# Accumulating products of a seven-product block in shared PSUM banks, with neighbouring blocks interleaved

## The chip, the cores and the metric

The kernel runs on one core of a Trainium2 chip. The metric is the time of one execution on the device in microseconds (us); lower is better. TensorE multiplies matrices into PSUM banks, VectorE and ScalarE do elementwise work and read PSUM, GpSimd does elementwise work in SBUF, and SyncE (SP) issues most of the transfers.

## The reference

Sliding-window attention (4 batches, 8 heads, 576 positions, window 64), and behind it two feed-forward parts on its 2,304 tokens. The change concerns only the second one's first product, which makes h.

```python
a = x @ w1;  b = x @ w2              # x: 2304 x 512 from attention
y = ((a * b) @ w3) @ w_out           # 2304 x 512
h = y @ w_in                         # 2304 x 2048
g = np.maximum(0.01 * h, h)
return g @ w_out2                    # 2304 x 512
```

## The kernel before, in words

Each float32 operand is split into a high part (fp32r) and a remainder, and `mm3` makes a product of three matmuls: high by high, high by low, low by high. Attention, the first feed-forward part and the loading of weights take the first half of the execution. y is kept transposed in DRAM (`yd`), and so is h (`hd`).

The stage of this study makes h. It is cut into 24 blocks (`Quad(p, c)`): p counts 8 pairs of 128 rows of features of h, c counts 3 pairs of 384 tokens. A block is a 2 x 2 product of submatrices, and it is made with seven products instead of eight, from sums and differences of the submatrices. `w_ops(p)` makes the seven weight operands (L553), `y_ops(c, j)` the seven operands of y (L527): loads, differences on VectorE, a cast to the high part on ScalarE (L574, L542), a subtraction for the low part on VectorE or, for the last c, on GpSimd (L575, L543). Blocks run in the order (0,0), (1,0), (2,0), (0,1), ... for the first three p, and then by p.

A product (`Quad.product`) is six matmuls of 128x128 by 128x384 into a PSUM bank of its own; eight banks take turns (six in `ps2`, two in `ps_h`). Then `Quad.add` carries the product to where it belongs: product 1 is copied by ScalarE (L608) into an SBUF tile `c`, and each other one is added by VectorE to a tile `c` (L610), seven additions in a block. Four tiles of a block are results, c11, c12, c21 and c22, and go to `hd` by SP (L615). The products come in the order 1, 6, 2, 7, 4, 5, 3. They are kept in their order on TensorE by `tc.issue_after(pss["pr"])`. On the other engines the order of the instructions is laid down when the kernel is built, by a scheduler with priorities (`first()` puts an instruction ahead) and its own estimate of times; each engine then runs its list strictly in order, and what is ready waits behind what is not.

Between products other work is put on the engines: `advance` takes the last weight matrix through its steps, two calls in a block while it lasts, of which ScalarE's part is a rescaling (L293, `f` from `raw`) that is put behind the last copy. `feed` loads the next piece on SP behind the last store of h. `w_ops` of a later p stands behind the fourth product of a block. After block 21 the pool `yb0` is released, and loads and splits for the last stage begin (`ahead`, L259, L693).

## Time and profile before

| what | us |
|---|---|
| median of three runs | 864.32 |
| runs | 864.15, 864.32, 867.67 |
| span of the profiled execution | 866.3 |
| TensorE busy, whole span | 821.0 |
| VectorE busy | 574.1 |
| ScalarE busy | 391.1 |
| granted clock of TensorE, mean | 0.988 |

The profile gives the span from the first to the last instruction of one execution. That execution's own time is not told apart from the three runs; 867.67, the only one above the span, has 1.4 us around it. TensorE's matmuls overlap: each is shown with 0.33 us in h's stage while the next starts after 0.17, so a wait shows as a larger distance between starts.

### The profile page before, as it was taken

The numbers are of one execution on the slowest core, as the hardware profiler recorded it, in microseconds if no ns is written. First come the engines' busy times: TensorE is split into PE (matmuls) and PEld (weight loads), VectorE is DVE, ScalarE is ACT, GpSimd is POOL, SyncE is SP. The second block draws the span as 40 slices with busy tenths as digits, with TensorE's granted clock in tenths as the row PEclk, the third lists the DMA queues.
The fourth block names the chain that finished last, engine by engine and source line by source line (L and its number), as shares of the span: only waits on it lengthen the run. The fifth ranks groups of instructions, "written<-read, shape, count | busy, mean of one in ns | idle before, by whom it ended". The sixth has DMA issues, their size and how long they took to land. (4 is left out here: it accounts for less than half of the span.)

```text
span 866.3 us, 15325 instructions
## 1 busy us (share of the span) xinstructions
PE 821.0 (95%) x5332; PEld 751.5 (87%) x5332; DVE 574.1 (66%) x1419; ACT 391.1 (45%) x988; POOL 82.8 (10%) x91
## 2 busy tenths in 40 slices
PE   5789799999999999999999799998999999999997
PEld 4577699999999999999999699997998888888885
DVE  6799996553655377657614987988768655555552
ACT  6687973333333254435324412322215545555552
POOL 1012551110111011100000330000000000000000
PEclk9999999999999999999999999999999999999999
DMA  8798787673546367874202447896638335344341
GB/s 248 198 218 237 198 204 197 152 156 76 130 107 147 68 158 194 242 223 134 77 29 64 147 156 254 284 287 227 209 130 284 112 98 158 105 130 131 98 129 45
DMA packets 203693, 139.44 MB, mean 161 GB/s; under 512 B 137312, under 2 KB 181856, under 8 KB 203616
## 3 DMA queue, kind: packets, MB, share of 16 engines
q1 hardware_dynamic: 199008, 133.74, 54.5%
q10 hardware_dynamic: 4608, 4.72, 1.7%
q8 instruction: 42, 0.69, 0.3%
q14 instruction: 35, 0.29, 0.1%
HBM read 94.63 MB, written 43.78 MB: 160 GB/s over the span
## 5 line engine op out<-in xcount | busy, mean ns | idle before, releaser
L75 PE MATMUL ab<-x,w 128*128 128x288 f32 x512 | 154.1, 301 | 4.8 <-ACT x L235 3.3
L76 PE MATMUL ab<-x,w 128*128 128x288 f32 x512 | 152.1, 297 | 0.0
L77 PE MATMUL ab<-x,w 128*128 128x288 f32 x512 | 152.1, 297 | 0.0
L75 PE MATMUL pr<-yop,w 128*128 128x384 f32 x324 | 111.0, 343 | 10.3 <-DVE c L610 7.3
L75 PE MATMUL o<-w,g 128*128 128x512 f32 x288 | 113.4, 394 | 0.5 <-ACT w L259 0.3
L76 PE MATMUL o<-w,g 128*128 128x512 f32 x288 | 113.1, 393 | 0.0
L77 PE MATMUL pr<-yop,w 128*128 128x384 f32 x324 | 109.5, 338 | 0.0
L76 PE MATMUL pr<-yop,w 128*128 128x384 f32 x324 | 109.4, 338 | 0.0
L75 PEld LDWEIGHTS ab<-x,w 128*128 128x128 f32 x512 | 97.1, 190 | 6.6 <-ACT x L235 3.5
L610 DVE TENSOR_TENSOR c<-pr,c 128x384 f32<-128x384 f32 x168 | 87.5, 551 | 18.7 <-PE pr L77 17.7
L76 PEld LDWEIGHTS ab<-x,w 128*128 128x128 f32 x512 | 97.2, 190 | 0.2
L77 PEld LDWEIGHTS ab<-x,w 128*128 128x128 f32 x512 | 97.1, 190 | 0.1
L694 DVE TENSOR_TENSOR t<-h,t 128x384 f32<-128x384 f32 x96 | 53.5, 558 | 49.2 <-ACT t L693 49.1
L77 PE MATMUL o<-w,g 128*128 128x512 f32 x288 | 82.8, 393 | 0.0
L75 PE MATMUL mm<-ab,wf 128*128 128x288 f32 x256 | 76.5, 310 | 0.0
L693 ACT ACTIVATE t<-h 128x384 f32<-128x384 f32 x96 | 50.5, 526 | 57.6 <-DVE g L696 55.0
L293 ACT ACTIVATE f<-raw 128x512 f32<-128x512 f32 x72 | 48.6, 674 | 60.7 <-DMA raw<-in_moe_w_out_dram 25.5
L77 PE MATMUL mm<-ab,wf 128*128 128x288 f32 x256 | 74.8, 294 | 0.0
L76 PE MATMUL mm<-ab,wf 128*128 128x288 f32 x256 | 74.6, 293 | 0.0
L75 PEld LDWEIGHTS pr<-yop,w 128*128 128x128 f32 x324 | 61.3, 189 | 14.8 <-DVE c L610 10.0
L696 DVE TENSOR_TENSOR g<-t,g 128x384 fp32r<-128x384 f32 x96 | 53.4, 557 | 28.0 <-ACT g L695 27.7
L192 POOL TENSOR_TENSOR s<-s,rs 128x384 f32<-128x384 f32 x48 | 41.5, 865 | 292.2 <-DVE rs L191 202.7
(100 smaller groups left out, 1541.1 us busy)
## 6 DMA issues: line engine op xcount, KB each, us to landing
hd<-c SPq DMA_DIRECT2D x96, 192.0 KB, 2.6
h<-hd SPq DMA_DIRECT2D x96, 192.0 KB, 2.4
raw<-in_moe_w_dram SPq DMA_DIRECT2D x32, 512.0 KB, 4.6
raw<-in_moe_w_out_dram SPq DMA_DIRECT2D x24, 512.0 KB, 4.8
raw<-in_moe_w_in_dram SPq DMA_DIRECT2D x16, 512.0 KB, 4.9
wd<-f SPq DMA_DIRECT2D x32, 256.0 KB, 3.3
f<-wd SPq DMA_DIRECT2D x32, 256.0 KB, 3.9
vt<-in_v_dram SPq DMA_DIRECT2D x56, 128.0 KB, 2.8
```

What stands on the lines that cost most here:

```text
L75: pe.matmul(ps, lhsT=lh, rhs=rh, start=first, stop=False)
L76: pe.matmul(ps, lhsT=lh, rhs=rl, start=False, stop=False)
L77: return pe.matmul(ps, lhsT=ll, rhs=rh, start=False, stop=last).ins
L192: pool.tensor_tensor(out=s, in0=s, in1=rs.unsqueeze(2).to_broadcast([P, GT, P]), op=ALU.mult)
L293: act.mul(u["f"], u["hi"].bitcast(F32), 2.0 ** -112)
L610: dve.tensor_tensor(out=self.sb[to], in0=ps, in1=self.sb[of], op=ALU.add)
L693: act.mul(t, h, 0.01)
L694: dve.tensor_tensor(out=t, in0=h, in1=t, op=ALU.max)
L696: dve.tensor_tensor(out=g[:, 1], in0=t, in1=f32(g[:, 0]), op=ALU.subtract)
```

## The change

Products 1, 6, 5 and 3 of a block now go one after the other into one bank (a) without clearing it, and ScalarE copies the partial sum out after each: 1 for c11, 1+6 for c21, 1+6+5 for c22, 1+6+5+3 for c12. Products 7 and 4 share a second bank (b), and product 2 has its own (c). VectorE adds three times in a block: 2 to c11, 7 to c22, 7+4 to c21. A product that writes on in a bank has to wait until the copy before it has been read out. The steps of neighbouring blocks are interleaved: seven product slots in a block, `ORDER` gives the slot of each step counted from the block's first, so that the sequence is 1, 2, 3 of the block before, 6, 7, 4 of the block before, 5. `w_ops` is called behind the fifth step and its last part behind the sixth; the weight tiles of p = 3 and 6 take the place of those of p = 0. `yb0` is released behind the last step of block 21.

```diff
@@ -71,10 +71,10 @@
 
         return tc.high_priority(offset=3000)
 
-    def mm3(ps, lh, ll, rh, rl, first, last):
-        pe.matmul(ps, lhsT=lh, rhs=rh, start=first, stop=False)
-        pe.matmul(ps, lhsT=lh, rhs=rl, start=False, stop=False)
-        return pe.matmul(ps, lhsT=ll, rhs=rh, start=False, stop=last).ins
+    def mm3(ps, lh, ll, rh, rl, first, last, more=False):
+        pe.matmul(ps, lhsT=lh, rhs=rh, start=first, stop=False, skip_group_check=more)
+        pe.matmul(ps, lhsT=lh, rhs=rl, start=False, stop=False, skip_group_check=more)
+        return pe.matmul(ps, lhsT=ll, rhs=rh, start=False, stop=last, skip_group_check=more).ins
 
     const = ctx.enter_context(tc.tile_pool(name="const", bufs=1))
     wpool = tc.alloc_tile_pool(name="wpool", bufs=1)
@@ -543,12 +543,12 @@
             (pool if c == NP - 1 else dve).tensor_tensor(out=t[:, i, j, 1], in0=x, in1=f32(t[:, i, j, 0]), op=ALU.subtract)
 
     def w_tile(p, j):
-        m = 1 if j == 3 else 2
-        if p:
-            return ph.tile([P, m, 2, 2 * P], F32R, name=f"w{j}", tag=f"w{j}", bufs=2)
+        shape = [P, 1 if j == 3 else 2, 2, 2 * P]
+        if p % 3 or p and j == 2:
+            return ph.tile(shape, F32R, name=f"w{j}", tag=f"w{j}", bufs=2)
         if j == 2:
-            return stage.tile([P, m, 2, 2 * P], F32R, name="raw", tag="raw", bufs=RAW)
-        return yb0.tile([P, m, 2, 2 * P], F32R, name=f"w{j}", bufs=1)
+            return stage.tile(shape, F32R, name="raw", tag="raw", bufs=RAW)
+        return yb0.tile(shape, F32R, name=f"w{j}", tag=f"w{j}", bufs=1)
 
     def w_ops(p):
 
@@ -564,9 +564,9 @@
         s1, s2, s3, s4 = (sums[i // 2][:, i % 2] for i in range(4))
         src = (u[1].rearrange("p k c m -> p c k m"), sums[0], sums[1], a11.unsqueeze(1))
         add, sub = ALU.add, ALU.subtract
-        ops = {}
-        for j, todo in ((3, ()), (1, ((s1, a21, a22, add), (s2, s1, a11, sub))), (0, ()),
-                        (2, ((s3, a11, a21, sub), (s4, a12, s2, sub)))):
+        ops = wop[p] = {}
+
+        def part(j, todo):
             for o, x0, x1, op in todo:
                 dve.tensor_tensor(out=o, in0=x0, in1=x1, op=op)
             t = w_tile(p, j)
@@ -575,7 +575,11 @@
             dve.tensor_tensor(out=l, in0=src[j], in1=f32(h), op=sub)
             for i in range(t.shape[1]):
                 ops[2 * j + i] = t[:, i]
-        wop[p] = ops
+
+        part(3, ())
+        part(1, ((s1, a21, a22, add), (s2, s1, a11, sub)))
+        part(0, ())
+        return lambda: part(2, ((s3, a11, a21, sub), (s4, a12, s2, sub)))
 
 
 
@@ -583,31 +587,39 @@
 
     n_of["bank"] = 0
 
+    def bank():
+
+        n_of["bank"] += 1
+        pool = ps_h if n_of["bank"] % 8 in (1, 2) else ps2
+        return pool.tile([P, DM], F32, name="pr")[:, 0:NB2]
+
     class Quad:
+
+        ORDER = (("a", 1, 0), ("c", 2, 1), ("a", 6, 3), ("b", 7, 4), ("a", 5, 6), ("a", 3, 9), ("b", 4, 12))
+
         def __init__(self, p, c):
             self.p, self.c = p, c
-            self.sb = {}
-
-        def product(self, m):
-            n_of["bank"] += 1
-            pool = ps_h if n_of["bank"] % 8 in (1, 2) else ps2
-            ps = pool.tile([P, DM], F32, name="pr")[:, 0:NB2]
+            self.sb, self.ps = {}, {}
+
+        def product(self, at, m):
+
+            new = at not in self.ps
+            if new:
+                self.ps[at] = bank()
             a, b = PRODUCTS[m]
             w, y = wop[self.p][a], yop[self.c]
             with tc.issue_after(pss["pr"]):
                 for j in range(2):
                     ws = slice(P * j, P * j + P)
-                    pss["pr"] = mm3(ps, w[:, 0, ws], w[:, 1, ws], y[:, b, j, 0], y[:, b, j, 1], j == 0, j == 1)
-            return ps
-
-        def add(self, to, ps, of):
-
-            if to not in self.sb:
-                self.sb[to] = ph.tile([P, NB2], F32, name="c", tag="c", bufs=8)
-            if of is None:
-                pss["copy"] = act.copy(self.sb[to], ps).ins
-            else:
-                dve.tensor_tensor(out=self.sb[to], in0=ps, in1=self.sb[of], op=ALU.add)
+                    pss["pr"] = mm3(self.ps[at], w[:, 0, ws], w[:, 1, ws], y[:, b, j, 0], y[:, b, j, 1], new and j == 0, j == 1, not new)
+            return self.ps[at]
+
+        def keep(self, to, ps):
+            self.sb[to] = ph.tile([P, NB2], F32, name="c", tag="c", bufs=8)
+            pss["copy"] = act.copy(self.sb[to], ps).ins
+
+        def add(self, to, ps):
+            dve.tensor_tensor(out=self.sb[to], in0=ps, in1=self.sb[to], op=ALU.add)
 
         def out(self, n):
             fh, th = int(n[1]) - 1, int(n[2]) - 1
@@ -615,14 +627,22 @@
             pss["store"] = sp.dma_start(hd[:, 2 * self.p + fh, t0:t0 + NB2], self.sb.pop(n)).ins
 
         def step(self, k):
-            m, adds, done = ((1, [("c11", None)], []), (6, [("c12", "c11")], []), (2, [("c11", "c11")], ["c11"]),
-                             (7, [("c22", "c12")], []), (4, [("c21", "c22")], ["c21"]),
-                             (5, [("c12", "c12"), ("c22", "c22")], ["c22"]), (3, [("c12", "c12")], ["c12"]))[k]
-            ps = self.product(m)
-            for to, of in adds:
-                self.add(to, ps, of)
-            for n in done:
-                self.out(n)
+
+            at, m, _ = self.ORDER[k]
+            ps = self.product(at, m)
+            if k in (0, 2, 4, 5):
+                self.keep({0: "c11", 2: "c21", 4: "c22", 5: "c12"}[k], ps)
+            if k == 1:
+                self.add("c11", ps)
+                self.out("c11")
+            if k == 4:
+                self.add("c22", self.ps["b"])
+                self.out("c22")
+            if k == 5:
+                self.out("c12")
+            if k == 6:
+                self.add("c21", ps)
+                self.out("c21")
 
     ysteps = []
     for b in range(B):
@@ -654,7 +674,7 @@
             ps_h = tc.alloc_tile_pool(name="ps_h", bufs=2, space=PSUM, side="right", reuse_waits="tile")
             yb0 = tc.alloc_tile_pool(name="yb0", bufs=1, side="right", reuse_waits="tile")
             yop[0] = yb0.tile([P, 7, 2, 2, NB2], F32R, name="yop")
-            early = [lambda: w_ops(0), lambda: y_ops(0, 0), lambda: y_ops(0, 1)]
+            early = [lambda: w_ops(0)(), lambda: y_ops(0, 0), lambda: y_ops(0, 1)]
     for e in ysteps:
         y_step(*e)
 
@@ -738,33 +758,35 @@
     FIRST = 3
     order = [(p, c) for c in range(NP) for p in range(FIRST)] + [(p, c) for p in range(FIRST, NF) for c in range(NP)]
     quads = [Quad(p, c) for p, c in order]
-    w_ops(1)
-    for i, q in enumerate(quads):
-        for k in range(7):
+    w_ops(1)()
+    slots_h = sorted((7 * i + Quad.ORDER[k][2], i, k) for i in range(len(quads)) for k in range(7))
+    for _, i, k in slots_h:
+        with first():
+            quads[i].step(k)
+        if k == 3 and order[i] == (NF - 2, NP - 1):
             with first():
-                q.step(k)
-            if k == 3 and order[i] == (NF - 2, NP - 1):
-                with first():
-                    for f in range(WLEAD):
-                        load_w(f)
-            if k in (1, 4) and i >= FIRST * (NP - 1) and n_of["fin"] < len(units):
-                if n_of["cap"] == KEPT:
-                    n_of["cap"], n_of["room"] = len(units), 3
-                    feed()
-                else:
-                    advance(len(units))
-            if k == 0 and i < FIRST * (NP - 1) and i % FIRST == 0:
-                c = i // FIRST + 1
-                yop[c] = ph.tile([P, 7, 2, 2, NB2], F32R, name=f"yop{c}", bufs=1)
-            if k == 3:
-                if i == 0:
-                    w_ops(2)
-                elif i < FIRST * (NP - 1) and i % FIRST in (1, 2):
-                    y_ops(i // FIRST + 1, i % FIRST - 1)
-                p = order[i][0] + 2 if order[i][1] == NP - 1 else 0
-                if FIRST <= p < NF:
-                    w_ops(p)
-        if order[i] == (NF - 1, 0):
+                for f in range(WLEAD):
+                    load_w(f)
+        if k in (1, 4) and i >= FIRST * (NP - 1) and n_of["fin"] < len(units):
+            if n_of["cap"] == KEPT:
+                n_of["cap"], n_of["room"] = len(units), 3
+                feed()
+            else:
+                advance(len(units))
+        if k == 0 and i < FIRST * (NP - 1) and i % FIRST == 0:
+            c = i // FIRST + 1
+            yop[c] = ph.tile([P, 7, 2, 2, NB2], F32R, name=f"yop{c}", bufs=1)
+        if k == 3:
+            if i == 0:
+                w_ops(2)()
+            elif i < FIRST * (NP - 1) and i % FIRST in (1, 2):
+                y_ops(i // FIRST + 1, i % FIRST - 1)
+        p = order[i][0] + 2 if order[i][1] == NP - 1 else 0
+        if k == 4 and FIRST <= p < NF:
+            rest = w_ops(p)
+        if k == 5 and FIRST <= p < NF:
+            rest()
+        if k == 6 and order[i] == (NF - 1, 0):
             yb0.release()
             po1 = tc.alloc_tile_pool(name="po1", bufs=4, side="right", reuse_waits="tile")
             for n in range(LOADS):
```

## Rows read from the trace of the kernel before

**Rows 1.** Timeline of TensorE, single rows: start, us taken, instruction, [idle before, releaser].

```profile
468.08 0.34 PE L75 MATMUL pr<-yop,w 128*128 128x384 f32 x1
...
476.55 0.34 PE L75 MATMUL pr<-yop,w 128*128 128x384 f32 x1
...
497.99 0.45 PE L75 MATMUL pr<-yop,w 128*128 128x384 f32 x1 [0.93 <-DVE c L610]
...
505.45 0.45 PE L75 MATMUL pr<-yop,w 128*128 128x384 f32 x1
...
579.43 0.33 PE L75 MATMUL pr<-yop,w 128*128 128x384 f32 x1
...
615.45 0.34 PE L75 MATMUL pr<-yop,w 128*128 128x384 f32 x1
...
659.24 0.34 PE L77 MATMUL pr<-yop,w 128*128 128x384 f32 x1
```

**Rows 2.** Stretches A to D: length, busy PE, PEld, DVE, ACT, POOL; PE clock, DMA share, GB/s.

```profile
468.10:505.50 37.40, 31.63 (x171) 28.70 (x169) 34.30 (x59) 19.66 (x43) 14.80 (x13) 1.00 0.48 153
505.50:549.40 43.90, 43.90 (x253) 43.90 (x253) 33.31 (x68) 9.02 (x17) 1.28 (x2) 1.00 0.68 229
549.40:615.40 66.00, 61.48 (x338) 59.92 (x337) 58.03 (x121) 17.29 (x32) 0.00 (x0) 0.97 0.82 262
615.40:659.40 44.00, 44.00 (x254) 43.86 (x252) 31.10 (x60) 11.63 (x24) 0.00 (x0) 1.00 0.55 181
```

**Rows 3.** Groups by line in h's stage: instructions, busy us, mean ns, idle before.

```profile
L75 PE MATMUL pr<-yop,w 128*128 128x384 f32 x324 | 111.0, 343 | 10.3 <-DVE c L610 7.3 <-ACT c L608 2.1 <-ACT io L520 0.9
...
L610 DVE TENSOR_TENSOR c<-pr,c 128x384 f32<-128x384 f32 x164 | 85.5, 551 | 18.7 <-PE pr L77 17.7 <-ACT f L293 0.4
...
L608 ACT COPY c<-pr 128x384 f32<-128x384 f32 x24 | 11.4, 474 | 39.4 <-PE pr L77 36.6 <-DMA hd<-c 2.8
```

**Rows 4.** Timeline of TensorE: a product's end, two waits, a longer matmul.

```profile
506.43 0.33 PE L77 MATMUL pr<-yop,w 128*128 128x384 f32 x1
...
555.24 0.44 PE L75 MATMUL pr<-yop,w 128*128 128x384 f32 x1 [0.45 <-ACT c L608]
...
605.42 0.44 PE L75 MATMUL pr<-yop,w 128*128 128x384 f32 x1 [2.09 <-DVE c L610]
...
607.29 0.53 PE L77 MATMUL pr<-yop,w 128*128 128x384 f32 x1
```

**Rows 5.** Timeline of ScalarE in the same stage, single rows.

```profile
485.78 0.47 ACT L608 COPY c<-pr 128x384 f32<-128x384 f32 x1
...
503.12 0.47 ACT L608 COPY c<-pr 128x384 f32<-128x384 f32 x1
...
506.81 0.48 ACT L608 COPY c<-pr 128x384 f32<-128x384 f32 x1 [1.33 <-PE pr L77]
...
554.72 0.47 ACT L608 COPY c<-pr 128x384 f32<-128x384 f32 x1
...
582.61 0.67 ACT L293 ACTIVATE f<-raw 128x512 f32<-128x512 f32 x1 [6.03 <-DMA wd<-f]
...
584.77 0.47 ACT L608 COPY c<-pr 128x384 f32<-128x384 f32 x1
...
645.05 2.19 ACT L259 CAST w<-f 128x512 fp32r<-128x512 f32 x4 [5.88 <-PE pr L77]
```

**Rows 6.** Waits, 468 to 506 us: us in total, times, longest.

```profile
ACT yop L542 <- DMA f<-yd: 9.3, 8, 2.0
...
ACT yop L542 <- DVE raw L540: 7.6, 9, 1.7
```

**Rows 7.** Waits, 549 to 616 us.

```profile
ACT f L293 <- DMA raw<-in_moe_w_out_dram: 14.2, 5, 4.6
...
ACT w L574 <- DMA f<-wd: 10.0, 4, 3.9
```

**Rows 8.** Instructions on tile c, 468.1 to 505.5 us: ns min/median/max, first and last.

```profile
L610 DVE TENSOR_TENSOR c<-pr,c x21: 541/545/551, 471.9 to 505.3; 128x384 f32<-128x384 f32 x21
```

## The prediction

> **What bounds it now.** I read the page of the profile first. TensorE is busy nearly throughout, so the end can move only by time in which it waits. The change touches one stage, that of h's products, from 468.08 us, where the first of 1,008 matmuls into `pr` starts, to 659.41, a matmul spacing after the last one starts [rows 1]. The table of stages [rows 2] is the next view: cut in four, the stage has TensorE idle in stretch A (31.63 of 37.40 us busy) and C (61.48 of 66.00) and never in B and D. To give the loss a size I took the starts of blocks from the timeline [rows 1]. The last six blocks (D) run undisturbed: from 615.45 to 659.24 are 251 steps of 0.1745 us, so a product takes 1.05 and a block of 42 matmuls 7.33. At that pace A (blocks 0 to 3, 37.37 us) loses 8.1; B and C (blocks 4 to 17, 110.00 us) lose 7.4, all of it in C, the last eight of them. The prize is thus 15.5 us, 1.8% of the kernel, and nothing else in the stage can shrink, since all 1,008 matmuls stay.
>
> Who is waited for is in the groups by line [rows 3]: before L75 TensorE waits mostly for VectorE's additions (7.3 us), less for ScalarE's copies (2.1); these 10.3 are less than 15.5 because each wait starts when the last matmul's modelled end is past, some 0.16 after the next could have started, and has 0.11 more behind it (0.44 instead of 0.33 us for the first matmul [rows 4]). VectorE is busy for 34.30 of 37.40 us in A and 58.03 of 66.00 in C: there it is nearly full. ScalarE is not (19.66 and 17.29), but it is often late: it stands in order behind instructions that wait [rows 5 to 7].
>
> **The engines' work.** Seven additions per block become three: 96 of 168 fall away, at 551 ns [rows 3] 52.9 us off VectorE. Four copies stand where one stood: 72 more at 474 ns, 34.1 us onto ScalarE. Over the four stretches VectorE goes from 156.7 to about 104, ScalarE from 57.6 to about 92 of 191.3. So the wait that dominates today loses its cause: in A VectorE needs 9 additions less by the end of block 3 (21 done today [rows 8], 12 then), at 545 ns some 4 to 5 us.
>
> **The wait that comes in.** Today a copy or an addition that is late stops TensorE only when eight banks are full, about seven products later. In the new order product 6 may not write bank a before ScalarE has copied product 1 from it, and so for 5 and 3. What this costs with ScalarE free: block 4's first product has its last matmul at 506.43, its end at 506.76, the copy at 506.81 [rows 4, 5], 0.05 later, for 0.48; from the copy that ends at 555.19 to the matmul at 555.24 is 0.05 again. So 0.91 us from the last start to the next permitted one, where 0.17 would do: 0.73 us lost if the next product follows at once. One product between covers 1.05 of it, and leaves 0.3 spare; two between, as nearly everywhere in the new order, leave 1.36. The price is therefore nothing if copies come within 1.36 us of their turn, and all that is beyond this if not.
>
> Rows bear on that. Block 1 starts at 476.55, so its first product is complete at 477.8; its copy runs at 485.78, 8.0 late. Block 3: 499.3 against 503.12, 3.9 late. Block 14: 580.7 against 584.77, 4.1 late, behind a rescaling that had waited 6.03 us for a store [rows 5]. Block 4 is on time. In A the ScalarE queue holds `y_ops`' casts, which wait 9.3 us for `yd` and 7.6 for VectorE's differences; in C rescalings and casts wait 14.2 and 10.0 us for loads [rows 6, 7]. Four times as many copies now stand in that queue, with 1.36 us where they had some seven.
>
> **Stretch by stretch.** A: were ScalarE's queue no faster than now, TensorE would at block 3 have to fall back from 3.9 behind to 1.36, that is 2.5 on top of today's 8.1: 10.6, the upper bound. Freed VectorE can give back 4 of this, through casts that wait for its differences; 6.6 then. Below stands 1, since in block 0 only one product lies between 1 and 6 and the copy has casts in front of it. I take 5.5, near the upper end, because the larger of the two waits is for a load that VectorE does not hasten alone. C: the lower bound is 1, if copies are put ahead of the late rescalings. The upper one is that blocks like 14 recur: 4.1 less 1.36 is 2.7 in four of the eight blocks, 11. I take 4: a stall of TensorE lets the transfers catch up, and the fall of the clock (below) goes with VectorE's longest wait, which caused it. B: raw loads begin in its last blocks; 0 to 2, I take 0.7. D: at the end 3 follows 5 at once, since no block is left to interleave: 0.73 and 0.11. Besides, `yb0` is released with ten products to go instead of fourteen (product 4 of block 21 comes later), 4.2 us later against the end; at that place ScalarE goes through four weight casts in 2.19 us [rows 5], and copies stand behind these and behind loads of h. 0.8 to 4, I take 2.1.
>
> Sum: 5.5 + 0.7 + 4 + 2.1 = 12.3 instead of 15.5, so 3.2 us less. The profiled span is 866.3 us, 2.0 above the median of the runs shown (864.32); carried to that median: 861.
>
> At nothing I put: the accumulation itself (a later product adds into a bank with the same matmuls); the order on TensorE, which a chain of issue edges pins, so that the interleaving is sure; the 96 stores, of which each block keeps four; the bank count (three a block; bank a is held for ten product times, and eight banks come round after 18); and `w_ops`. Of this (for p = 3) the part for products 7 and 3 waits for product 3 of block 7 and is next used nine products, 9.4 us, later; in between stand two differences, a cast and a subtraction. Its two loads are issued three products later than now. If that cover is gone, TensorE waits for `w`, some 2.5 us at a time, the mean of the four waits for these loads [rows 7]. VectorE's addition of 7 into c22 has five products before 4 writes the same bank. Behind a late copy stand, on ScalarE, the next rescaling and its load's turn; on SP, the h stores and the raw loads that follow them.
>
> **A rule against it.** Row: after the longest wait, 2.09 us before 605.42, a matmul at 607.29 takes 0.53 instead of 0.33 us [rows 4], and the mean granted clock of C is 0.97 [rows 2]: about 4 us (0.03 of 66 over a half) at 1.2 instead of 2.4 GHz, 2 us lost. The shorter waits in A, 0.93 among them [rows 1], leave the clock at 1.00. The Trainium skill, "TensorE: Matmul & The Clock Gate", section "A second HAM failure mode: psum-queue depth-cycling", says that short idle moments between groups that cycle through PSUM banks can make the clock swing between its levels and cost more than the idle time. By that rule a kernel with several short waits per block would lose clock again and again; by the rows it does so after a long one only.
>
> **Rivals.** Faster to the full: the copies find their place in ScalarE's order and only block 0 and the end cost something, 1.5 + 0 + 1 + 1 = 3.5; 12 less, 852. For it: ScalarE is under half busy and VectorE's queue empties. Against: the rows of late copies. 0.20.
>
> Slower, TensorE locked to ScalarE: the copies stay as late as today and each lateness counts. A 10.6, C 11, B 1, D 2.5: 25.1, that is 9.6 more, 874. It decides once one copy in each of the twelve blocks of A and C comes over 2.4 us behind its turn, since (15.5 less 2.8 for B and D) over 12 is 1.06, and 1.36 is spare. For it blocks 1, 3 and 14; against it VectorE's relief, and that C's transfers are paced by the stores themselves. 0.19.
>
> The clock swings: one fall of 2 us in every third block, eight in all, 16 on top of the forecast: 877. The one fall in the trace against the many short waits without one speaks against it. 0.05.
>
> Even swap: additions' waits become copies' waits, one for one: 864 to 867. 0.06.
>
> Forecast: partly recovered, 856 to 865, 0.50.
>
> **Chances.** This kernel's measurement tells about 0.5% (4.3 us) from no change, so faster means below 860.0. Of the forecast's 0.50 about 0.21 lies there and 0.29 within; full recovery adds 0.20 to faster; the even swap adds 0.06 to the same, the locked case 0.01; the rest is slower: 0.41, 0.36, 0.23. The range goes from 850, near full recovery, to 873, where the locked case begins to be complete; some 0.04 lies below and 0.14 above.
>
> **What would show it.** Right: additions 72, copies 96, VectorE near 104 us in the stage; the waits before L75 named for ScalarE's copies rather than VectorE's; A shorter by 2 to 3 us, C by 3; a last wait of about 0.7 before the end. Wrong towards fast: copies on ScalarE waiting for TensorE nearly everywhere, and blocks of 7.33 us throughout. Wrong towards slow: idle time of TensorE over 20 us in the stage, its releaser the copy, and ahead of the copy a cast or rescaling that waits for a load; or a granted clock below 0.95.

## The result, and the profile after

The changed kernel is slower: 871.93 us in the median of 20 runs against 866.45 for the kernel before, a ratio of 1.0061 with a 95% interval of 1.0044 to 1.0077. The forecast was 861.0 and faster, 0.996 of the 864.32 that stood for the kernel before. The time lies inside the forecast's range of 850 to 873, but it moved the other way.

The profiled execution took 873.67 us, 1.7 above that median; its span is 871.9, against 866.3 before. The stage of h's products now lasts from 468.81 to 664.24 us. The first rows are TensorE's timeline, with the last two matmuls across the end of the stage.

```profile
472.19 0.44 PE L75 MATMUL pr<-yop,w 128*128 128x384 f32 x1 [1.13 <-ACT c L619]
...
502.70 0.44 PE L75 MATMUL pr<-yop,w 128*128 128x384 f32 x1 [2.34 <-ACT c L619]
...
504.07 0.52 PE L75 MATMUL pr<-yop,w 128*128 128x384 f32 x1
...
554.47 0.44 PE L75 MATMUL pr<-yop,w 128*128 128x384 f32 x1 [1.55 <-ACT c L619]
...
661.60 0.44 PE L75 MATMUL pr<-yop,w 128*128 128x384 f32 x1 [1.54 <-ACT c L619]
...
664.07 0.34 PE L77 MATMUL pr<-yop,w 128*128 128x384 f32 x1
...
665.53 0.50 PE L75 MATMUL o<-w,g 128*128 128x512 f32 x1 [1.12 <-DVE c L622]
```

Against 0.1745 us for a matmul, as in the prediction, the 28, 42, 56 and 42 products of A to D lose 9.4, 3.0, 4.2 and 3.0 us: 19.6, where the kernel before lost 15.5 [rows 1, 2] and the forecast had 12.3. With 0.7 us more before the stage and 0.8 more between its end and the output stage this makes the 5.6 us between the spans. The table of stages, in the columns of [rows 2]:

```profile
468.80:507.40 38.60, 32.60 (x170) 30.68 (x169) 30.71 (x49) 23.99 (x55) 16.46 (x14) 0.96 0.54 169
507.40:554.40 47.00, 44.68 (x254) 43.76 (x252) 23.93 (x48) 17.51 (x37) 0.00 (x0) 1.00 0.65 222
554.40:617.20 62.80, 60.03 (x336) 58.50 (x337) 41.87 (x82) 26.57 (x56) 0.00 (x0) 1.00 0.80 267
617.20:664.20 47.00, 45.02 (x254) 43.93 (x252) 18.86 (x34) 19.33 (x41) 0.00 (x0) 1.00 0.47 163
```

VectorE is relieved everywhere, 115 us instead of 157, and the fall of the clock has gone from C. But TensorE now idles in B and D as well, which had been free, and the clock falls in A. The groups by line and the waits of the stage, against [rows 3, 6, 7]:

```profile
L75 PE MATMUL pr<-yop,w 128*128 128x384 f32 x324 | 111.4, 344 | 12.9 <-ACT c L619 12.8
...
L619 ACT COPY c<-pr 128x384 f32<-128x384 f32 x96 | 45.0, 477 | 56.3 <-PE pr L77 55.7 <-DMA f<-wd 0.5
L622 DVE TENSOR_TENSOR c<-pr,c 128x384 f32<-128x384 f32 x72 | 39.8, 554 | 58.2 <-PE pr L77 46.7 <-ACT c L619 11.4
```

```profile
ACT f L293 <- DMA raw<-in_moe_w_out_dram: 20.4, 10, 3.4
...
ACT w L574 <- DMA f<-wd: 10.5, 9, 3.5
...
ACT yop L542 <- DMA f<-yd: 8.2, 8, 1.9
```

No wait before L75 is named for VectorE's additions any more, and 12.8 us are named for ScalarE's copies. What stands ahead of a late copy is read in ScalarE's timeline, here ahead of the waits at 502.70, 554.47 and 661.60:

```profile
500.48 0.51 ACT L542 CAST yop<-raw 128x384 fp32r<-128x384 f32 x1 [0.55 <-DVE raw L540]
501.75 0.51 ACT L542 CAST yop<-raw 128x384 fp32r<-128x384 f32 x1 [0.76 <-DVE raw L540]
502.17 0.47 ACT L619 COPY c<-pr 128x384 f32<-128x384 f32 x1
...
552.87 0.66 ACT L293 ACTIVATE f<-raw 128x512 f32<-128x512 f32 x1 [3.45 <-DMA wd<-f]
553.43 0.60 ACT L574 CAST w<-raw 128x512 fp32r<-128x512 f32 x1
553.94 0.48 ACT L619 COPY c<-pr 128x384 f32<-128x384 f32 x1
...
660.16 0.61 ACT L259 CAST w<-f 128x512 fp32r<-128x512 f32 x1
660.66 0.52 ACT L713 ACTIVATE t<-h 128x384 f32<-128x384 f32 x1
661.09 0.46 ACT L619 COPY c<-pr 128x384 f32<-128x384 f32 x1
```

Each of these copies had its data for some time. In A the copy stood behind casts that waited for VectorE's differences, at the end of B behind a rescaling that waited for a transfer. In D it stood behind a weight cast and a step of the output stage (L713) that ran one after the other without a wait; the product it copies had ended at about 660.1, and there the next product of bank a follows at once. After 502.70 the clock falls: ten matmuls follow each other by 0.32 instead of 0.17 us, 1.5 us more.

### The profile page after: what moved, and what is told of

It is laid out like the page before. It is cut to its first block, busy times and chain, and to the rows that moved or that the text cites. A ratio compares the mean times of both kernels' runs of the same rounds, so it can differ in the third digit from the quotient of the medians.

```text
span 871.9 us, 15303 instructions
## 1 busy us (share of the span) xinstructions
PE 821.3 (94%) x5332; PEld 751.2 (86%) x5332; DVE 530.5 (61%) x1323; ACT 421.2 (48%) x1060; POOL 83.7 (10%) x91
## 4 chain that ended last, share of the span: by engine, by line
PE 67%; DMA 17%; DVE 6%; ACT 5%; issue 2%; SPq 1%; POOL 0%; ACTq 0%; DVEq 0%; POOLq 0%
PE o L75 7%; PE o L76 7%; PE o L77 7%; PE ab L75 7%; PE ab L77 6%; PE ab L76 6%; DMA raw<-in_moe_w_dram 5%; PE mm L75 4%; PE pr L75 3%; PE pr L77 3%; PE mm L76 3%; PE pr L76 3%; PE mm L77 3%; PE sc L175 3%; DMA raw<-in_moe_w_out_dram 2%
## 5 line engine op out<-in xcount | busy, mean ns | idle before, releaser
L75 PE MATMUL ab<-x,w 128*128 128x288 f32 x512 | 153.7, 300 | 6.0 <-ACT x L235 3.2
L75 PE MATMUL pr<-yop,w 128*128 128x384 f32 x324 | 111.4, 344 | 12.9 <-ACT c L619 12.8
L75 PE MATMUL o<-w,g 128*128 128x512 f32 x288 | 113.3, 394 | 1.4 <-DVE c L622 1.1
L75 PEld LDWEIGHTS ab<-x,w 128*128 128x128 f32 x512 | 96.7, 189 | 7.9 <-ACT x L235 3.4
L75 PEld LDWEIGHTS pr<-yop,w 128*128 128x128 f32 x324 | 61.4, 189 | 17.9 <-ACT c L619 17.4
L75 PE MATMUL mm<-ab,wf 128*128 128x288 f32 x256 | 76.5, 310 | 0.0
L713 ACT ACTIVATE t<-h 128x384 f32<-128x384 f32 x96 | 50.4, 526 | 51.9 <-DVE g L716 51.3
L622 DVE TENSOR_TENSOR c<-pr,c 128x384 f32<-128x384 f32 x72 | 39.8, 554 | 58.2 <-PE pr L77 46.7
L293 ACT ACTIVATE f<-raw 128x512 f32<-128x512 f32 x72 | 48.7, 677 | 48.9 <-DMA raw<-in_moe_w_out_dram 25.1
L619 ACT COPY c<-pr 128x384 f32<-128x384 f32 x96 | 45.0, 477 | 56.3 <-PE pr L77 55.7
```

The source lines that it names most:

```text
L75: pe.matmul(ps, lhsT=lh, rhs=rh, start=first, stop=False, skip_group_check=more)
L293: act.mul(u["f"], u["hi"].bitcast(F32), 2.0 ** -112)
L619: pss["copy"] = act.copy(self.sb[to], ps).ins
L622: dve.tensor_tensor(out=self.sb[to], in0=ps, in1=self.sb[to], op=ALU.add)
L713: act.mul(t, h, 0.01)
```

## The experiments

All ratios are to the kernel before, run on the same chip. The losses are those of the profiled execution, worked out as above; since the profiled execution of a kernel lies up to 6.7 us from the median of its runs (e14), a ratio weighs more than a sum. Kernels with the same source in a stretch show how far such a loss scatters: A lost 6.6 to 9.4 us in the five that leave the work of A as in the changed kernel (changed, e6, e9, e11, e15); in the seven that leave it so in B and C (changed, e5, e9, e10, e11, e15, e18) B lost 1.5 to 3.2 and C 3.0 to 5.9.

| kernel | ratio (95% interval) | A, B, C, D: us lost | sum |
|---|---|---|---|
| before | 1 | 8.1, 0, 7.4, 0 | 15.5 |
| changed | 1.0061 (1.0044 to 1.0077) | 9.4, 3.0, 4.2, 3.0 | 19.6 |
| e1, more distance | 1.0111 (1.0082 to 1.0140) | 10.5, 4.9, 2.2, 3.7 | 21.3 |
| e2, no interleaving | 1.047 (1.043 to 1.051) | 16.8, 10.4, 16.8, 10.7 | 54.6 |
| e3, interleaving alone | 1.0046 (1.0028 to 1.0064) | 7.9, 0.1, 7.2, 0.2 | 15.4 |
| e4, copies on VectorE | 1.0210 (1.0173 to 1.0246) | 10.4, 1.7, 9.5, 6.4 | 28.0 |
| e5, casts of y moved | 1.0022 (1.0002 to 1.0042) | 3.8, 3.0, 4.2, 4.6 | 15.6 |
| e6, rescalings moved | 1.0082 (1.0048 to 1.0116) | 8.8, 0.5, 3.9, 4.5 | 17.7 |
| e7, e5 and e6 | 1.0041 (1.0012 to 1.0069) | 5.6, 1.7, 6.6, 4.4 | 18.3 |
| e8, e7 on the kernel before | 1.0009 (0.9981 to 1.0036) | 6.8, 0.8, 5.3, 0 | 12.9 |
| e9, old end | 1.0062 (1.0037 to 1.0087) | 8.9, 1.8, 3.0, 0.1 | 13.8 |
| e10, e5 and e9 | 0.9995 (0.9975 to 1.0014) | 5.6, 2.6, 3.7, 0.1 | 12.0 |
| e11, old block 21 | 1.0042 (1.0021 to 1.0064) | 7.7, 1.6, 4.8, 3.5 | 17.6 |
| e12, e7, e9, casts of w from p = 2 | 1.0029 (1.0008 to 1.0050) | 9.7, -0.1, 2.9, 0.1 | 12.6 |
| e13, the same from p = 3 | 0.9953 (0.9927 to 0.9979) | 3.9, 0.4, 3.8, 0.1 | 8.2 |
| e14, e13, banks turned | 0.9982 (0.9956 to 1.0007) | 3.9, 0.6, 0.3, 0.1 | 4.9 |
| e15, e9, banks turned | 1.0054 (1.0033 to 1.0074) | 6.6, 3.2, 4.8, 0.1 | 14.7 |
| e16, e13's moves on the kernel before | 0.9953 (0.9935 to 0.9971) | 5.5, 1.2, 3.9, 0.1 | 10.7 |
| e17, e13 without the old end | 1.0023 (1.0001 to 1.0045) | 5.8, 0.2, 7.8, 3.9 | 17.7 |
| e18, subtractions alone | 1.0021 (0.9999 to 1.0044) | 4.2, 1.5, 5.9, 3.2 | 14.8 |

**Distance between the products of one bank.** The queue theory says that copies come late behind ScalarE instructions that wait. Then more products between two uses of a bank help (e1), and none between them hurts at once (e2).

```diff
-        ORDER = (("a", 1, 0), ("c", 2, 1), ("a", 6, 3), ("b", 7, 4), ("a", 5, 6), ("a", 3, 9), ("b", 4, 12))
+        ORDER = (("a", 1, 0), ("c", 2, 2), ("a", 6, 4), ("b", 7, 3), ("a", 5, 8), ("a", 3, 12), ("b", 4, 13))   # e1
+        ORDER = (("a", 1, 0), ("c", 2, 1), ("a", 6, 2), ("b", 7, 3), ("a", 5, 4), ("a", 3, 5), ("b", 4, 6))     # e2
```

> Slots of a block are 1:0, 2:2, 7:3, 6:4, 5:8, 3:12, 4:13, so that three products instead of two lie between those that write on in bank a. Queue theory (a product waits because the copy before it stands in ScalarE's queue behind something late, by what exceeds the cover of the products between): the cover grows by one product, 1.05 us, so of the waits that the changed kernel shows those under 1.05 vanish and the others shrink by 1.05; the stage's loss of 19.5 us against 7.33 a block falls to some 6, the kernel ends about 13 us before the changed one, ratio to the kernel before 0.985 to 0.995. Data theory (loads and buffers of the stage are late by themselves and the copies only carry the name): no gain, ratio about 1.006. Interleaving theory (what costs is that blocks overlap and that the later w_ops and the later release follow): overlap grows, ratio 1.006 to 1.015.

> Slots 1:0, 2:1, 6:2, 7:3, 5:4, 3:5, 4:6: the banks are shared as in the change, but blocks follow one another. Queue theory: 3 follows 5 at once, 0.84 us in each of 24 blocks, 20 in all, and one product between 1 and 6 and between 6 and 5 leaves 0.3 us of cover instead of 1.36, so that lateness counts 1 us more at each of the dozen late copies: 25 to 40 us above the changed kernel, ratio to the kernel before 1.03 to 1.05. Interleaving theory: without overlap the changed kernel's loss goes, ratio 1.00 or below. Data theory: about as the changed kernel, plus the 20 us of the adjacent products at most.

e2 came as the queue theory expected: in 18 of the 24 blocks, where nothing else disturbs, product 3 loses 0.73 to 0.79 us behind product 5, beside the 0.73 of the prediction; in the other six it loses more. One of the 18:

```profile
512.00 0.45 PE L75 MATMUL pr<-yop,raw 128*128 128x384 f32 x1 [0.61 <-ACT c L619]
```

e1 missed. C fell to 2.2, but A rose: with more distance the order of ScalarE's list put block 0's second copy, that of 1+6, behind seven casts of `y_ops` (478.73, the third row), and TensorE waited 5.96 us for it before product 5. B rose too, with a wait of 2.53 us for a weight cast. Here distance helped only against lateness that the order did not take back. The ratio lies in the range of the interleaving theory, but e2, without overlap, is much slower, and e3 below, with the overlap alone, loses no more in the stage than the kernel before.

```profile
474.35 0.51 ACT L542 CAST yop<-f 128x384 fp32r<-128x384 f32 x1 [0.94 <-DMA f<-yd]
...
476.76 0.51 ACT L542 CAST yop<-f 128x384 fp32r<-128x384 f32 x1 [1.50 <-DMA f<-yd]
...
478.73 0.47 ACT L619 COPY c<-pr 128x384 f32<-128x384 f32 x1
```

```profile
479.25 0.69 PE L75 MATMUL pr<-yop,w 128*128 128x384 f32 x1 [5.96 <-ACT c L619]
```

**The parts of the change.** e3 keeps the interleaving and the later `w_ops`, but gives each product its own bank and VectorE its seven additions. e4 keeps the shared banks and gives the 96 copies to VectorE.

```diff
-            pss["copy"] = act.copy(self.sb[to], ps).ins
+            dve.tensor_copy(self.sb[to], ps)                # e4
```

> Each product has a bank of its own again, with one copy on ScalarE and seven additions on VectorE per block, but the order of the products, the points of w_ops and of the release and the weight tiles are those of the change. Queue theory: the copies no longer stop TensorE, VectorE is as full as before; ratio 0.997 to 1.004, with the waits named for VectorE's additions. Interleaving theory: the loss of the change stays, ratio 1.005 or more.

> The changed kernel with the four copies of a block on VectorE instead of ScalarE. Lag theory (each engine runs a list fixed at build time; on the chip the loads and what waits for them come later than the list assumes, and a product that writes on in a bank is tied to whichever list its copy stands in): VectorE's list has y_ops' differences and the last weights' bit operations, which wait for ScalarE's casts and rescalings, so the stage still loses 15 to 25 us, ratio to the kernel before 1.000 to 1.012, the waits named for L619 on VectorE. ScalarE theory (only ScalarE's queue is late): the stage loses under 8, ratio 0.985 to 0.992.

In e3 the stage is as before the change, so the new losses of B and D belong to the shared banks. Its ratio is 1.0046 all the same, at the edge between its two expectations: behind the stage the profiled execution takes 5.7 us longer than before, 3.99 of them a wait for an operand of the output stage that comes late. `yb0` is released ten products before the end there, not fourteen; that this is the reason was not tried by itself.

```profile
668.62 0.50 PE L75 MATMUL o<-w,g 128*128 128x512 f32 x1 [3.99 <-ACT g L708]
```

e4 is worse than the changed kernel and beyond the range of the lag theory; 16.8 us of its waits are named for VectorE's copies. So it is not ScalarE's queue alone that can be late.

**Taking the waiting work from ScalarE.** e5 puts `y_ops`' casts on GpSimd (except for c = 0) and, to make room there, the subtractions for the last c on VectorE. e6 moves the rescalings, e7 both, e8 both on the kernel before.

```diff
-            act.copy(t[:, i, j, 0], x)
-            (pool if c == NP - 1 else dve).tensor_tensor(out=t[:, i, j, 1], in0=x, in1=f32(t[:, i, j, 0]), op=ALU.subtract)
+            (pool.tensor_copy if c else act.copy)(t[:, i, j, 0], x)
+            dve.tensor_tensor(out=t[:, i, j, 1], in0=x, in1=f32(t[:, i, j, 0]), op=ALU.subtract)    # e5
...
-                act.mul(u["f"], u["hi"].bitcast(F32), 2.0 ** -112)
+                if now["scale"] < KEPT:
+                    act.mul(u["f"], u["hi"].bitcast(F32), 2.0 ** -112)
+                else:
+                    pool.tensor_scalar(u["f"], u["hi"].bitcast(F32), 2.0 ** -112, None, op0=ALU.mult)    # e6
```

> The changed kernel, but the casts of y_ops for the second and third c run on GpSimd and all their subtractions on VectorE, so that in the first stretch (468 to 507 us) ScalarE has hardly anything before its copies. Queue theory: the stretch's loss of 9.4 us falls to some 3 (block 0, with one product between 1 and 6, stays), no fall of the clock there, the kernel 5 to 7 us faster than the changed one, ratio to before 0.998 to 1.001. Data theory: the stretch loses as much, and TensorE's waits are now named for yop (GpSimd's casts or VectorE's subtractions).

> The changed kernel with the 16 rescalings of the last weight on GpSimd. Lag theory: from 507 to 617 us ScalarE has only w_ops' casts in front of its copies, and the 7.2 us lost there fall to 2 or 3; before 507 nothing changes; 4 us less than the changed kernel, ratio to before 1.000 to 1.004. Data theory (late loads stop the stage by themselves): as the changed kernel, 1.006.

> The changed kernel with y_ops' casts for the second and third c and the 16 rescalings on GpSimd, all of y_ops' subtractions on VectorE. Lag theory: the two gains add, the stage loses some 9 us (3 or 4 in block 0 and with VectorE, 2 or 3 in the middle, 3 at the end) instead of 19.5, ratio to the kernel before 0.993 to 0.998. Data theory: as the changed kernel or slower, 1.006 or more.

> The kernel before, own banks and seven additions, with the same moves to GpSimd as the run beside it. Lag theory: VectorE was its bound in the two stretches that lose, it gets 14 more subtractions in the first, and ScalarE's lists did not count: ratio 0.999 to 1.006, slower than the changed kernel with these moves. If it is as fast as that one, sharing the banks is worth nothing by itself.

e5 took A from 9.4 to 3.8 us, as expected; its ratio came down by less than expected, to 1.0022. e6 brought no time in the median (expected 1.000 to 1.004, measured 1.0082), and e7 missed its expectation: with the rescalings gone the copies stood behind `w_ops`' casts, which wait for loads (rows of e7: ScalarE, and then TensorE; in this kernel the copy is L622).

```profile
572.22 0.41 ACT L577 CAST w<-f 128x256 fp32r<-128x256 f32 x1 [4.97 <-DMA f<-wd]
574.98 0.62 ACT L577 CAST w<-f 128x512 fp32r<-128x512 f32 x1 [2.35 <-DMA f<-wd]
575.50 0.85 ACT L622 COPY c<-pr 128x384 f32<-128x384 f32 x2
```

```profile
576.02 0.69 PE L75 MATMUL pr<-yop,w 128*128 128x384 f32 x1 [4.03 <-ACT c L622]
```

e8, the same moves on the kernel before, does not differ from that kernel (1.0009). It was expected to be slower than e7 and is not: with these two moves the shared banks gain nothing either.

**The end.** e9 and e10 give blocks 21 to 23 the old form (own banks, seven additions, no interleaving; `yb0` again released with fourteen products to go), on the changed kernel and on e5. e11 does this for block 21 alone.

```diff
-    quads = [Quad(p, c) for p, c in order]
+    quads = [(Old if i >= 21 else Quad)(p, c) for i, (p, c) in enumerate(order)]     # e11: i == 21
```

> The last three blocks (21 to 23) go back to a bank for each product, seven additions and no interleaving; blocks 0 to 20 stay as changed, and yb0 is released with fourteen products to go, as before the change. Theory that the end of the stage costs by itself (late release, adjacent products, copies behind the weight casts): blocks 18 to 23 lose under 1 us instead of 3.0, the matmuls of the output stage begin 0.5 us after the last product instead of 1.3, the stage loses 16 to 18 instead of 19.6, ratio to the kernel before 1.000 to 1.003. Rival, that the loss of the end was only carried there from earlier stretches or is chance: ratio 1.005 to 1.007 as the changed kernel, with the loss in another place.

> The old form for blocks 21 to 23, and besides the casts of y_ops on GpSimd as in the run before it that moved them. If the two costs (waiting casts in A, the end of the stage) stand side by side: A 4, B 3, C 4, D under 1, sum 12, ratio 0.996 to 0.999. If what is won at one place is lost at the next wait for a load: 1.001 to 1.004.

> Only block 21 in the old form, so that yb0 is released with fourteen products to go, but blocks 22 and 23 interleaved with shared banks. If the late release is what the end costs: as with all three in the old form, D under 1.5. If it is the shared banks at the end (adjacent products, copies behind weight casts): D 2 to 3 and an output stage that begins over 1 us after the last product, ratio 1.004 to 1.006.

The traces do what the theory said of D: 0.1 us with the old form, 3.5 with block 21 alone, so the loss is that of the shared banks and not of the late release. Part of it comes back at once: the output stage waits 1.99 us in e9 for the last additions. The medians agree for e10, 0.0027 below e5 with intervals that overlap, and not for e9, which missed its expectation and stands where the changed kernel stood; its profiled execution was the fastest of its eight, 3.6 us under their median.

**Copies alone.** e12 also puts the casts of `w_ops` on GpSimd from p = 2 on, which leaves ScalarE little but copies until D. e13 leaves p = 2, whose casts fall into A, on ScalarE. e14 and e15 are e13 and e9 with the ring of banks turned by four places.

```diff
-            act.copy(h, src[j])
+            (pool.tensor_copy if p > 1 else act.copy)(h, src[j])     # e12; p > 2 in e13, e14, e16, e17
...
+    for _ in range(4):
+        ps2.tile([P, DM], F32, name="pr")     # e14, e15: ahead of w_ops(1)()
```

> Rescalings, the casts of y_ops and, from p = 2 on, of w_ops run on GpSimd, and blocks 21 to 23 have the old form: in the stage ScalarE has little else than the copies to do until the weight casts of D. Theory that TensorE waits because copies stand behind ScalarE instructions that wait for loads: copies come on time from block 4 on, waits of L75 for ScalarE under 4 us, A 3 to 4, B and C together under 3, D under 1, sum 5 to 8, ratio 0.988 to 0.994. Rival, that the operands themselves (loads, GpSimd at 1.5 us an instruction) come late and would stop TensorE whatever stands ahead of the copies: waits for GpSimd or VectorE take their place, sum 14 or more, ratio 0.998 or more.

> As the run with the copies alone on ScalarE, but the four casts of w_ops(2), which fall into A, are on ScalarE again. If GpSimd's fuller queue made the operands of A late: A 4 to 6 as in the runs that moved only the casts of y_ops, B 0, C 3, D 0, output stage 2 after the last product, ratio 0.993 to 0.998. If the loads are the bound of A whatever casts them once copies are on time: A 8 to 10, ratio 1.000 to 1.004.

> The same, and the ring of PSUM banks turned by four at the start of the stage, so that the first tile of the output stage falls on the bank that is free first, as before the change. If the wait of 2 us at the start of that stage is the bank: it begins 0.3 to 0.7 us after the last product, and the ratio is 0.0015 below that of the run without the turn. If it is VectorE's queue or a weight, the wait stays.

> The changed kernel with blocks 21 to 23 in the old form and the ring of banks turned by four. If the end was what is left beside late copies: D 0.1, output stage under 0.7 us after the last product, 4 us less than the changed kernel, ratio 1.001 to 1.003. If the median stays at 1.006 the end is not where the median's loss lies, and other executions lose elsewhere what the profiled one does not show.

In e12 the copies wait for TensorE, and not TensorE for them, from the second block on, and B and D lose nothing. But it missed its expectation (1.0029): A lost 9.7, now to operands, with waits of 2.21 and 2.95 us for `yop` and a fall of the clock behind them. e13 keeps A at 3.9 and is the first kernel faster than before, by 0.5%. Its waits of the stage (L622 is the copy, L577 `w_ops`' cast, L545 that of `y_ops`):

```profile
ACT c L622 <- PE pr L77: 111.2, 76, 5.4
...
POOL w L577 <- DMA f<-wd: 12.9, 7, 3.7
```

```profile
L75 PE MATMUL pr<-yop,w 128*128 128x384 f32 x324 | 109.9, 339 | 5.1 <-DVE c L625 3.7 <-ACT c L622 1.3
```

The waits for loads are still there, but GpSimd has them, and TensorE's waits for copies fell from 12.8 to 1.3 us; 3.7 are left for VectorE's additions. The turned banks did nothing for the wait at the output stage's start (1.97 us in e14, 2.00 in e15, for VectorE's last additions), and e15's 1.0054 stays by the changed kernel, the second of its two cases. Why this wait is 0.3 us, and for a weight cast, in the kernel before stays open; it does not hang on the form of the end alone, since e8 has 2.16 with the same end and e16 none. e14's 0.9982 does not differ from e13's 0.9953 by more than the intervals.

**Whose gain it is.** e16 makes e13's moves on the kernel before; e17 makes them on the changed kernel with its own end.

> The kernel before, with the casts of y_ops, those of w_ops from p = 3 on and the rescalings on GpSimd. If the shared banks win once ScalarE is free: VectorE stays the bound of A and C here, the stage loses 11 to 15 us, ratio 0.998 to 1.002, above the 0.9953 of the same move on the changed kernel. If the moved work alone made the gain: the stage loses 8 or less, ratio 0.994 to 0.997.

> The changed kernel with the same three moves and its own interleaved end. If the end costs what the profiles show (D 3 to 4.5 against 0.1, less the longer wait at the start of the output stage): 2 to 3 us above the run with the old form at the end, ratio 0.998 to 1.000. If the end is worth nothing in the median: 0.994 to 0.997.

e16 has the ratio of e13, 0.9953, as expected of moved work alone, though its stage loses 10.7 us and not 8 or less. So the gain belongs to the moved work; the shared banks add nothing to it that can be measured. e17 came out above both of its ranges: with the changed kernel's own end the gain is lost. e16 is the simplest version whose ratio lies under those of both kernels. On the kernel before, the casts of `y_ops`, the rescalings and the subtractions together (e8) brought nothing that can be measured; with the casts of `w_ops` on top (e16) the gain came. The two ran on different chips, but their intervals do not meet.

**The confounded edit.** e5 had moved two things in A, and the trace of the changed kernel shows why the smaller may count: from 486.42 us on GpSimd subtracts, and from then on VectorE's operations between SBUF tiles are longer (VectorE, L543 and L540; L622 reads PSUM).

```profile
486.01 0.55 DVE L622 TENSOR_TENSOR c<-pr,c 128x384 f32<-128x384 f32 x1
486.48 1.37 DVE L543 TENSOR_TENSOR yop<-raw,yop 128x384 fp32r<-128x384 f32 x1
487.77 0.55 DVE L622 TENSOR_TENSOR c<-pr,c 128x384 f32<-128x384 f32 x1
...
493.52 1.37 DVE L540 TENSOR_TENSOR raw<-f,raw 128x384 f32<-128x384 f32 x1
494.81 0.55 DVE L622 TENSOR_TENSOR c<-pr,c 128x384 f32<-128x384 f32 x1
```

e18 changes this alone in the changed kernel.

```diff
-            (pool if c == NP - 1 else dve).tensor_tensor(out=t[:, i, j, 1], in0=x, in1=f32(t[:, i, j, 0]), op=ALU.subtract)
+            dve.tensor_tensor(out=t[:, i, j, 1], in0=x, in1=f32(t[:, i, j, 0]), op=ALU.subtract)
```

> The changed kernel with one edit: the fourteen subtractions of y_ops for the last c run on VectorE instead of GpSimd; the casts stay on ScalarE. The run that moved the casts to GpSimd made this edit too. While GpSimd subtracts, VectorE's differences (L540) take up to 1.37 us instead of 0.55, and ScalarE's casts wait for them. If this is what makes the copies of blocks 2 and 3 late: differences 0.55 us throughout, A 4 to 6 instead of 9.4, ratio 1.001 to 1.004. If the casts' place in ScalarE's queue and their loads do it: A 8 to 10 and ratio 1.005 to 1.007.

The differences are back at 0.55 us, the waits of casts for them are gone from the list, A loses 4.2, under the 6.6 to 9.4 of the kernels that leave A as it was, and the ratio is that of e5, 1.0021 beside 1.0022; its interval just reaches that of the changed kernel. The differences by line, in the kernel before, in the changed kernel and in e18, and stretch A of e18:

```profile
L540 DVE TENSOR_TENSOR raw<-f,raw 128x384 f32<-128x384 f32 x8 | 7.4, 923 | 1.9 <-DMA f<-yd 1.9
...
L540 DVE TENSOR_TENSOR raw<-f 128x384 f32<-128x384 f32 x8 | 7.0, 879 | 0.0
```

```profile
L540 DVE TENSOR_TENSOR raw<-f,raw 128x384 f32<-128x384 f32 x8 | 6.8, 850 | 2.2 <-DMA f<-yd 2.2
L540 DVE TENSOR_TENSOR raw<-f 128x384 f32<-128x384 f32 x8 | 6.5, 817 | 0.8 <-DMA f<-yd 0.7
```

```profile
L540 DVE TENSOR_TENSOR raw<-f 128x384 f32<-128x384 f32 x8 | 4.4, 554 | 0.0
L540 DVE TENSOR_TENSOR raw<-f,raw 128x384 f32<-128x384 f32 x8 | 4.4, 553 | 1.4 <-DMA f<-yd 1.4
```

```profile
469.20:503.00 33.80, 30.93 (x174) 29.64 (x173) 29.94 (x62) 23.52 (x55) 0.00 (x0) 1.00 0.60 187
```

What the casts' place in the queue was thought to do in A was thus mostly done by GpSimd's subtractions: through the slow differences they made the casts late, and through these the copies. ScalarE is as busy as before (23.52 us), and its copies come in time.

## Why the prediction was wrong, point by point

**In sum.** The forecast left 12.3 us of loss in the stage, and 19.6 were measured. Of the 7.3 between them A has 3.9, B 2.3, D 0.9 and C 0.2; another 1.5 lie just before and behind the stage, for which the prediction had no term. The wait itself was foreseen, copies that stand behind late ScalarE instructions; what failed is the share of it that the freed VectorE was to give back.

**The prize and the relief of VectorE: right, but mis-sized.** The waits for additions vanished. VectorE came to 115 us, not 104: a removed addition was priced at 551 ns, while additions in a row follow each other by 0.47, as three in a row of 1.48 us in the trace of before show (the row below). By an estimate from these, 96 times 0.08 us, that is some 8 of the 11. ScalarE came to 87, near the 92.

```profile
504.85 1.48 DVE L610 TENSOR_TENSOR c<-pr,c 128x384 f32<-128x384 f32 x3
```

**A: the step that failed.** The prediction took 6.6 as the loss that is left when "freed VectorE can give back 4 of this, through casts that wait for its differences", and chose 5.5. Measured are 9.4. The casts' waits for differences did shrink, from 7.6 to 2.7 us, but the differences themselves stayed slow (the 16 of them took 13.3 us beside 14.4 before and 8.8 in e18), and the copies behind the casts were late enough to use up the 1.36 us that are spare and to stop TensorE for 2.34 us more in block 3, with a fall of the clock behind it. That VectorE was "nearly full" in A was read off as work that the change removes; part of it was stretched instructions that the change does not touch. Without the stretch (e18) A loses 4.2, near the 5.5.

**B: mis-sized.** 0.7 was taken from a range that ended at 2; 3.0 were lost. The late rescalings and weight casts begin before the cut between B and C, and the copies behind them count there too. e6 (0.5) and e12 to e14 (-0.1 to 0.6), which take that work out of ScalarE's queue, show that the mechanism is the queue.

**C: right, the size partly by luck.** 4.2 beside 4, without the fall of the clock, behind rescalings and weight casts that wait for transfers, as the rows of late copies had said. With the same source there C lost 3.0 to 5.9 in other kernels. The fall in the kernel before had cost 1.5 us (ten matmuls 0.32 us apart), not the 2 that were worked out from the mean clock.

**D and the end: short by 1.7 us.** 2.1 was taken; D lost 3.0, and the output stage's start 0.8 more, which had no term. The two reasons given, adjacent products and copies behind weight casts, are in the trace; a late operand, as the late release may bring it, shows only in e3. What the end is worth in the median stays open: e13 against e17 says 0.7%, e5 against e10 0.3%, the changed kernel against e9 and e15 nothing. The profiled executions of e9 and e15 lay 3.6 and 3.9 us under their medians and that of e17 5.6 above, so these traces do not show where the others lost. In the medians only A's part is confirmed (e5, e18); those of B and D are read from the traces alone.

**Costs put at nothing.** These held for the accumulation, the order on TensorE and `w_ops`: no wait for `w` shows, and no bank but a was waited for at length.

**The rivals.** The lock of TensorE to ScalarE is what happened in kind, in thirteen waits and not in every block, with 19.6 us lost instead of 25.1. The swing of the clock did not come: after the change the profiled execution falls once in the stage, after its longest wait, though there were thirteen. The Trainium skill's rule ("TensorE: Matmul & The Clock Gate", "A second HAM failure mode: psum-queue depth-cycling") agrees with some rows and not with others. At the stage's end the clock fell after two waits of 0.81 to 1.36 us less than 3 us apart in e5, e6, e7 and e17; at the stage's start two waits of 1.13 and 0.60 us, 2.9 us apart, left it at its full level in the changed kernel.

## What to carry to other kernels

Moving work off a full engine can turn its late results into late results of the engine that takes over; ask first what stands ahead of the new work in that engine's list and what it waits for, and give it to a queue in which nothing waits. Before calling an engine full, compare the durations of its instructions with those of the same form elsewhere in the trace: a stretched instruction can be a neighbour's doing, and one line (e18) undid here about two thirds of what the whole change had cost. And make the same side move on the kernel before (e16), or its gain is put down to the change.

## What the runs showed of the hardware

GpSimd slows VectorE. While GpSimd runs a subtraction between SBUF tiles (1.0 to 1.4 us each), VectorE's subtractions between SBUF tiles take up to 1.37 us instead of 0.55, while its additions that read one operand from PSUM stay at 0.55 (0.54 to 0.56 from 486 us on in stretch A of the changed kernel). In e5, where GpSimd casts instead (0.5 to 0.8 us), they take up to 0.88. The Trainium skill, "SBUF — State Buffer", section "Who interferes with whom", says that a VectorE instruction with two SBUF inputs contends with a GpSimd instruction that reads SBUF, and one with at most one SBUF input, outside certain modes, does not; the rows agree on both. It holds in the kernel before, too (up to 1.41 us), and was not looked for. Whether e18's edit alone speeds up the kernel before was not tried.

The clock of TensorE fell (matmuls 0.32 us apart instead of 0.17, for 1.6 to 5.5 us) after single waits of 1.81 us (e18) to 5.96 us (e1), but not after each of them: 2.42 us in e13 and 2.38 in e11 left it at its full level.
